# Attention with a batch's rounds of sums in one place, three exponentials a group, three score buffers in a fixed turn

## The chip, the cores and the metric

The kernel runs on one core of a Trainium2 chip. The metric is the device time of one execution in microseconds (us), lower is better. In the text PE or TensorE is the matrix engine, ACT or ScalarE does the exponentials, DVE or VectorE and POOL or GpSimd do element-wise work, and SP's queue issues most transfers.

## The reference

Attention for 8 batches of 12 heads, 448 positions, head size 64, with scores capped by a tanh; then a mixture of eight experts, each of which takes 448 of the 3584 tokens by a greedy assignment of the gate's logits.

```
scores = (q @ k.T) / 8
scores = cap * tanh(scores / cap)          # cap is 30
attn   = exp(scores - max);  attn /= sum(attn)
out    = attn @ v                          # per head; x = out as (3584, 768)
logits = x @ w_gate                        # 8 experts, at most 448 tokens each, in order of logit
y      = relu(x[mask] @ w1[e]) @ w2[e]     # per expert
```

## The kernel before, in words

All of it is one program whose order on every engine is written by hand: each engine carries out its instructions in the order in which the Python code emits them. Attention comes first (about the first 305 us), then the routing and the experts. The change touches attention only.

Attention goes through 24 **groups** g of four heads, three to a batch: b is the batch of the group and m (0, 1, 2) its place in it. One pass of the loop over g is a **step**. The 448 keys are cut into seven **blocks** r of 64. A step issues:

- `qk(g,r)`, in the order strings `Qr`: eight score matmuls (line 148) into a buffer `psS` of two PSUM banks, and a tanh on ACT (line 159) from there to a tile `e`. There are two such buffers. The exponential (line 164) works in place on `e`, one for the blocks (0,1), one for (2,3), one for (4,5) and one for block 6 (`GRP`); it is put behind the next block's tanh.
- `avq(g-1,r)`, `Ar`: eight matmuls (line 196) that multiply the weights of the group before by v and add up in `psA`, of which there is one. `av_out` (line 210) copies it to `xT` on DVE, and the next group's A0 waits for that copy.
- `esum`: DVE adds the `e` tiles of a group to `es` (line 170): `e1` at the end of the group's own step, `e2` and `r6` a step later. What is left are two halves; they are added by `r0` on DVE for the last group of a batch, and for the other two by `halves` on POOL (line 357), ahead of which a one-element copy `pin` (line 356) reads the newest `es`, so that it waits for DVE's sum.
- `rounds`: matmuls of `xT` with the gate's columns and of `es` with ones (line 219), 32 columns of the array each. They give the logits of batch b-1 and its sums. There are three rounds a batch: `R0` in step m=0, `R1` in step m=1, `R2` in step m=2 (for batch 0, four in the same three places).
- after the last round `logit_in` and `sums` (lines 254 to 264), a step later `ltr` (four transpositions on PE, line 290), `logit` (lines 301 to 309) on DVE and `heads` (line 326) on POOL.
- for the batch two back, `turn` (a DVE transposition, line 271) and `scale` (POOL, line 278), whose result goes to HBM.
- `tr`: two DVE transpositions that make the next group's `tk` and `tq` (line 133), without which its Q0 can't start.

`ORDER`, `EARLY`, `BEFORE` and `FINAL` (lines 348 to 351) say in which order blocks, rounds and the last batch's extra work (`T0`, `T4`, `W`, `L`) come. The small accumulators (`misc` and `side` of the rounds, the transposed logits) have two PSUM banks of their own, `psM`.

Of the kernel before, what the change touches and what calls it, by code (L numbers as in the profile page):

```python
# [8 lines left out]
PSUM=bass.MemoryType.PSUM  # L9
# [7 lines left out]
EB=3  # L17
def attention(nc, tc, c1, xp, pM, ep, nl, pT, q, k, v, cap, w_gate, xs, L1, ident, on_logits, on_turn, NDEF, setup, mark):

# [4 lines left out]
    N=B*NQ  # L24
# [23 lines left out]
    with ExitStack() as ctx:  # L48
# [4 lines left out]
        c2=ctx.enter_context(tc.tile_pool(name="c2",bufs=1))  # L53
        pS=ctx.enter_context(tc.tile_pool(name="pS",bufs=2,space=PSUM))

# [30 lines left out]
        nc.scalar.activation(tb,ident[:,0:1],AF.Tanh)  # L86
        ips=pM.tile([128,512],F32,name="psM")
        def idle(n):
# [41 lines left out]
        def tr(g,part,lo=0,hi=HG):  # L130
            if g>=N: return
            if lo==0: tks[g,part]=tp.tile([128,HG,S],F32,name="t"+"kq"[part])
            nc.vector.transpose(tks[g,part].rearrange("p m s -> p (m s)")[:,lo*S:hi*S],nats[g,part][:,lo*NB:hi*NB,:].rearrange("p k d -> p (k d)"))
        GRP=((0,1),(2,3),(4,5),(6,)); LOC={r:(gi,n) for gi,rs in enumerate(GRP) for n,r in enumerate(rs)}
        def ev(g,r):
# [4 lines left out]
        def qk(g,r):  # L140
            gi,n=LOC[r]
            if n==0: eh[g,gi]=ep.tile([128,len(GRP[gi]),2,S],F32,name=f"e{gi}")
            ps=pS.tile([128,2,512],F32,name="psS")
            if g:
                for o in range(2):
                    for h in range(2):
                        hp=slice(h*64,h*64+64)
                        nc.tensor.matmul(ps[o*64:o*64+64,h,:S],tks[g,0][hp,o,r*64:r*64+64],tks[g,1][hp,o,:],start=True,stop=True)  # L148
            elif r<6:
                o,u=divmod(r,3)  # L150
                for h in range(2):
                    hp=slice(h*64,h*64+64)
                    for c in range(2): nc.tensor.matmul(ps[c*64:c*64+64,h,:S],tks[g,0][hp,o,u*128+c*64:u*128+c*64+64],tks[g,1][hp,o,:],start=True,stop=True)
            else:
                for o in range(2):
                    for h in range(2):
                        hp=slice(h*64,h*64+64); w=64*(1-o)
                        nc.tensor.matmul(ps[w:w+64,h,:S],tks[g,0][hp,o,384:448],tks[g,1][hp,o,:],start=True,stop=True)
            nc.scalar.activation(ev(g,r),ps[:,:,:S],AF.Tanh,scale=sr[0])  # L159
            e=eh[g,gi]  # L160
            while wait: wait.pop(0)()
            if g==N-1 and gi>=2: e=ev(g,r)
            elif n<len(GRP[gi])-1: return
            act=lambda: nc.scalar.activation(e,e,AF.Exp,scale=sr[1],bias=bias)  # L164
            if g==N-1 and gi>=2: act()
            else: wait.append(act)
        def esum(g,what):
            if not 0<=g<N: return
            if what=='e1': es_t[g]=es.tile([128,2,2,S],F32,name="es",bufs=4)
            t=es_t[g]; add=lambda o,a,b: nc.vector.tensor_tensor(o,a,b,op=ALU.add)  # L170
            if g==0 and what in ('e1','e2'):
                o=int(what[1])-1
                add(t[:,o],ex(g,o,0),ex(g,o,1)); add(t[:,o],t[:,o],ex(g,o,2))
            elif g==0:
# [4 lines left out]
            elif what=='e1': add(t,eh[g,0],eh[g,1])
            elif what=='e2': add(t,t,eh[g,2])  # L180
            else:
                r=int(what[1])
                add(t[:,0],t[:,0],ev(g,r) if r else t[:,1])
        avp={}; pair=[None]
# [26 lines left out]
        def rnd(b,*ns,of=None):  # L211
            of=of or (ROUNDS if b else FIRST)
            for n in ns:
                for q,t,a,c,k in of[n]:
                    bank=(misc,side)[k]
                    if b not in bank: bank[b]=pM.tile([128,512],F32,name="psM")
                    rhs=xT[b][:,c,:] if t is gw else es_t[b*NQ+c[0]][:,c[1],c[2],:]
# [4 lines left out]
        def turn_v(lo,hi):  # L222
            if not lo:
# [3 lines left out]
                for o in range(2): nc.gpsimd.memset(vt['g'][o*64:o*64+64,:,:,16+o:17+o],1.0)  # L227
            ps=pM.tile([128,512],F32,name="psM")
            for r in range(lo,hi): nc.tensor.transpose(ps[:,(r-lo)*128:(r-lo+1)*128],nats[N-1,2][:,r].rearrange("p h d -> p (h d)"),ident)
            nc.vector.tensor_copy(vt['t'][:,lo*128:hi*128],ps[:,:(hi-lo)*128])  # L230
        def gate_v():
            ps=pM.tile([128,512],F32,name="psM")
            for r in range(7):
# [7 lines left out]
        def logit_v(b,of,t,under):  # L241
            lg=xp.tile([128,S],F32,name="lgt",bufs=1)
            nc.scalar.activation(lg,of[:,:S],AF.Copy)
            under()
            ps=pM.tile([128,512],F32,name="psM")
            for j in range(NJ): nc.tensor.matmul(ps[:CP,j*36:j*36+36],lg[:,j*CP:(j+1)*CP],fold,start=True,stop=True)
# [7 lines left out]
        def logit_in(b,p0=0):  # L254
            lgs[b]=xp.tile([128,S],F32,name="lg",bufs=1)
            nc.vector.tensor_copy(lgs[b][p0:],misc.pop(b)[p0:,:S])
            if b in side:
                nc.vector.tensor_tensor(lgs[b][64:],lgs[b][64:],side.pop(b)[:64,:S],op=ALU.add)
# [26 lines left out]
        def ltr(b,what=0,pool=None):  # L285
            p0=64 if what==2 else 0; W=128-p0
            lg=lgs.pop(b)
            ps=pM.tile([128,512],F32,name="psM") if pool is None else pool
            for j in range(NJ):
# [57 lines left out]
        part=None  # L347
        ORDER=["Q2 A0 Q3 Q4 A1 A2 A3 Q5 Q6 A4 A5 A6","Q2 R1 A1 Q3 Q4 A2 A3 Q5 Q6 A4 A5 A6","Q2 A1 A2 Q3 Q4 R2 A3 Q5 Q6 A4 A5 A6"]
        EARLY=["Q2 Q3 Q4 I2 Q5 I4 Q6 I16","Q2 A1 A2 Q3 Q4 Q5 A3 A4 Q6 A5 A6"]
        BEFORE="Q2 A1 Q3 R1 Q4 T0 A2 Q5 A3 A4 Q6 T4 A5 A6"  # L350
        FINAL="Q2 A1 R2 Q3 Q4 A2 L A3 Q5 A4 W Q6 A5 A6"
        HELD=lambda g: g==N-2 or 0<=g<N and 0<g//NQ<B-1 and g%NQ<2
        pin=c1.tile([1,1],F32,name="pin")
        def halves(g,last):
            if not HELD(g): return
            if last is not None: nc.gpsimd.tensor_copy(pin,es_t[last][0:1,0,0,0:1])
            nc.gpsimd.tensor_tensor(es_t[g][:,0],es_t[g][:,0],es_t[g][:,1],op=ALU.add)
        RNO=({"R0":(0,1),"R1":(2,),"R2":(3,)},{"R0":(0,),"R1":(1,),"R2":(2,)})
        def rounds(bb,m,n):
            rnd(bb,*RNO[bb>0][n])  # L360
            if m==2:
                logit_in(bb)
                if bb<B-NDEF: sums(bb)
        for g in range(N):
# [6 lines left out]
            last=g==N-1  # L371
            order=g>=G2; first=bb==0; old=bb-1 if m==0 and 0<=bb-1<B-NDEF else None
            qk(g,0)
            if old is not None: ltr(old)
            if m==0 and bb>=0: rounds(bb,m,"R0")
            qk(g,1)
            av_out(g-2)
            if g and (m or g<G2): avq(g-1,0)
            stored()
            if m: halves(g-4+m,g-1)  # L380
            if old is not None: logit(old); heads(old)
            if m==0 and bb>1: on_turn(bb-2)
            turn(b-2,m); scale(b-2,m)
            two=(0,1) if m==1 else (1,0)
            tr(g+1,two[0] if order else 0)
            if order: tr(g+1,two[1])
            if m==1 and bb>0: on_logits(bb-1)
            for w in ('e2','r') if g==1 else ('e2','r6'): esum(g-1,w)
            if g>1 and not HELD(g-1): esum(g-1,'r0')
            if last: halves(N-2,None)  # L390
            if not order: tr(g+1,1)
            for t in (EARLY[g] if g<2 else FINAL if last else BEFORE if g==N-2 else ORDER[m]).split():
                if t[0]=='R': bb>=0 and rounds(bb,m,t)
                elif t=='L': logit(bb); on_logits(bb)
                elif t[0]=='I': idle(int(t[1:]))
                elif t=='T0': turn_v(0,4)
                elif t=='T4': turn_v(4,7)
                elif t=='W': gate_v()
                else: (qk if t[0]=='Q' else lambda g,r: avq(g-1,r))(g,int(t[1]))
            if not last: esum(g,'e1')  # L400
        av_out(N-2)
        stored()
        g=N-1; b=B-1
        LAST=[RA,RB]
        two=pS.tile([128,2,512],F32,name="psS")
        part_v(two[:,0],0,1)
# [21 lines left out]
class Routing:  # L428
# [198 lines left out]
    def search(s,wp,turned=()):  # L627
# [473 lines left out]
def full(nc,tc,q,k,v,cap,wg,w1,w2,out):  # L1101
    with ExitStack() as ctx:
# [63 lines left out]
```

## Time and profile before

| what | value |
|---|---|
| three runs | 858.77, 858.78, 859.48 us; median 858.78 |
| the profiled execution | 858.0 us, its span from the first to the last instruction 856.2 |
| busy share of the span | PE 98%, DVE 68%, ACT 67%, POOL 54% |
| attention | about 0 to 305 us |

The shares are means over attention and experts. In attention ACT, DVE and PE are all near full. The profiled execution's own time (858.0) is 0.78 below the median of the runs. TensorE's granted clock is full in all of it.

### The profile page before, as it was taken

Reading aid. Unit: us, or ns where it says so; the run is one execution under the profiler, and the core shown is the slowest. Engines: PE = TensorE matmul, PEld = TensorE weight load, DVE = VectorE, ACT = ScalarE, POOL = GpSimd, SP = SyncE. Lnnn points to the kernel's source line nnn. Section 1 sums busy time; section 2 is a strip of 40 time slices with the busy share of each in tenths; the row PEclk is TensorE's granted clock in tenths of the full one; section 3 lists DMA queues with packets and bytes.
Section 4 is the critical chain, followed back from the end, with each engine's and each line's share of the span. In section 5 each row is a group of like instructions: output and inputs, shape, how many; then the busy total and the mean of one; then the engine's idle time right before and its main releaser. Section 6 shows DMA issues by size and latency. Waiting matters only on the chain.

```text
span 856.2 us, 17676 instructions
## 1 busy us (share of the span) xinstructions
PE 840.2 (98%) x6109; PEld 614.5 (72%) x6109; DVE 580.4 (68%) x1907; ACT 572.4 (67%) x832; POOL 462.5 (54%) x637
## 2 busy tenths in 40 slices
PE   8999999999999998999999999999999999999997
PEld 5333333333333357889889989989899899999997
DVE  3878899999989778667777777777757780230110
ACT  6999999999999753562764755737727725525521
POOL 8203336346333235573673864856856856837931
PEclk9999999999999999999999999999999999999999
DMA  8999999888995107716706917927928828838601
GB/s 126 137 142 148 157 158 156 159 160 158 154 152 125 23 2 226 229 36 189 222 16 193 311 42 209 317 58 207 308 56 211 288 65 232 257 118 234 202 10 56
DMA packets 364249, 133.70 MB, mean 156 GB/s; under 512 B 290592, under 2 KB 357472, under 8 KB 364160
## 3 DMA queue, kind: packets, MB, share of 16 engines
q1 hardware_dynamic: 354656, 102.27, 55.5%
q0 software_dynamic: 4656, 22.02, 7.5%
q10 hardware_dynamic: 4848, 8.29, 2.9%
q8 instruction: 48, 0.79, 0.4%
q14 instruction: 41, 0.34, 0.1%
HBM read 94.40 MB, written 30.08 MB: 145 GB/s over the span
## 4 chain that ended last, share of the span: by engine, by line
PE 76%; issue 7%; DVE 5%; SPq 5%; DMA 4%; POOL 2%; ACT 1%; POOLq 0%; ACTq 0%; DVEq 0%
PE psH L1002 25%; PE psH L1033 20%; PE psA L196 13%; PE psS L148 12%; SPq L83 3%; PE psM L219 2%; DVE es L170 2%; DMA xg<-xs,idx 1%; DVE cmpD L605 1%; POOL w2l L884 1%; DMA k<-in_k_dram 1%; DMA w1r<-in_moe_w_dram 1%; PE psX L826 1%; PE psM L290 1%; SPq L867 1%
## 5 line engine op out<-in xcount | busy, mean ns | idle before, releaser
L1033 PE MATMUL psH<-w2h,hh 128*128 128x384 f32 x896 | 235.3, 340 | 0.0
L1033 PE MATMUL psH<-w2l,hh 128*128 128x384 f32 x512 | 166.5, 340 | 0.5 <-POOL gap L882 0.5
L1033 PEld LDWEIGHTS psH<-w2h,hh 128*128 128x128 f32 x896 | 161.8, 188 | 0.3
L164 ACT ACTIVATE e<-e,bias 128x1792 f32<-128x1792 f32 (+1 forms) x97 | 158.5, 1636 | 0.1
L159 ACT ACTIVATE e<-psS 128x896 f32<-128x896 f32 x168 | 150.5, 956 | 11.1 <-PE psS L148 7.1
L1002 PE MATMUL psH<-xgh,w1h 128*128 128x448 f32 x384 | 143.2, 373 | 0.3 <-ACT xgh L962 0.3
L1002 PE MATMUL psH<-xgh,w1l 128*128 128x448 f32 x384 | 141.5, 369 | 0.0
L148 PE MATMUL psS<-tq,tk 64*64 64x448 f32 x1288 | 139.3, 538 | 1.1 <-ACT e L159 1.1
L884 POOL TENSOR_TENSOR w2l<-w2r,w2h 128x768 fp32r<-128x768 f32 x64 | 118.1, 1846 | 37.5 <-ACT w2h L880 30.5
L1002 PE MATMUL psH<-xgl,w1h 128*128 128x448 f32 x384 | 136.8, 369 | 0.0
L196 PE MATMUL psA<-e,nv 64*64 64x448 f32 x1232 | 131.9, 539 | 1.0 <-DVE xT L210 1.0
L884 POOL TENSOR_TENSOR w1l<-w1r,w1h 128x768 fp32r<-128x768 f32 x62 | 114.2, 1843 | 19.7 <-ACT w1h L880 15.3
L148 PEld LDWEIGHTS psS<-tq,tk 64*64 64x64 f32 x1288 | 47.5, 132 | 75.4 <-issue 47.0
L196 PEld LDWEIGHTS psA<-e,nv 64*64 64x64 f32 x1232 | 44.8, 133 | 73.8 <-issue 64.3
L1033 PEld LDWEIGHTS psH<-w2l,hh 128*128 128x128 f32 x512 | 95.6, 188 | 1.5 <-POOL gap L882 1.4
L1008 ACT ACTIVATE hh<-psH 128x448 fp32r<-128x448 f32 x64 | 34.8, 544 | 86.4 <-PE psH L1002 80.1
L1010 DVE SCALAR_TENSOR_TENSOR hh<-psH,hh 128x64 fp32r<-128x64 f32 (+1 forms) x128 | 44.0, 386 | 67.8 <-ACT hh L1008 66.7
L1039 ACT ACTIVATE on<-psH 128x384 f32<-128x384 f32 x48 | 23.4, 487 | 88.5 <-PE psH L1033 82.5
L170 DVE TENSOR_TENSOR es<-es,e 128x896 f32<-128x896 f32 (+2 forms) x48 | 77.7, 1619 | 2.5
L909 POOL DMA_INDIRECT xg<-xs,idx x32 | 34.3, 1073 | 81.2 <-DVE zz L774 64.8
L1002 PEld LDWEIGHTS psH<-xgh,w1h 128*128 128x128 f32 x384 | 72.5, 189 | 5.8 <-ACT xgh L962 0.5
L1002 PEld LDWEIGHTS psH<-xgh,w1l 128*128 128x128 f32 x384 | 72.3, 188 | 5.3
(390 smaller groups left out, 1339.1 us busy)
## 6 DMA issues: line engine op xcount, KB each, us to landing
w1r<-in_moe_w_dram SPq DMA_DIRECT2D x128, 192.0 KB, 4.7
w2r<-in_moe_w_dram SPq DMA_DIRECT2D x64, 384.0 KB, 6.5
k<-in_k_dram SPq DMA_DIRECT2D x92, 112.0 KB, 3.8
q<-in_q_dram SPq DMA_DIRECT2D x92, 112.0 KB, 4.0
nv<-in_v_dram SPq DMA_DIRECT2D x88, 112.0 KB, 3.3
xs<-xw SPq DMA_DIRECT2D x72, 112.0 KB, 2.6
xz<-pl ACTq DMA_DIRECT2D x18, 384.0 KB, 3.3
xs<-xn SPq DMA_DIRECT2D x1, 1344.0 KB, 6.5
```

The lines of the kernel that those rows point to most:

```text
L83: (nc.scalar if first and a else nc.sync).dma_start(z[w:w+32,lo*NB:hi*NB,:],src[b,h0+2*t+lo:h0+2*t+hi,:,a*32:a*32+32].rearrange("h (k s) d ...
L148: nc.tensor.matmul(ps[o*64:o*64+64,h,:S],tks[g,0][hp,o,r*64:r*64+64],tks[g,1][hp,o,:],start=True,stop=True)
L159: nc.scalar.activation(ev(g,r),ps[:,:,:S],AF.Tanh,scale=sr[0])
L164: act=lambda: nc.scalar.activation(e,e,AF.Exp,scale=sr[1],bias=bias)
L170: t=es_t[g]; add=lambda o,a,b: nc.vector.tensor_tensor(o,a,b,op=ALU.add)
L196: nc.tensor.matmul(avp[g,o][h*64:h*64+64,:S],z[hp,r,h,:],ev(g,r)[hp,h,:],start=r==0,stop=r==6)
L884: (eng or nc.gpsimd).tensor_tensor(view(l),r,view(h).bitcast(F32),op=ALU.subtract)
L909: g=nc.gpsimd.indirect_dma_start(out=row(j,n),out_offset=None,in_=xs,in_offset=bass.IndirectOffsetOnAxis(ap=res[p][0][:n,j:j+1],axis=0))
L1002: nc.tensor.matmul(ps[:,:C],a[:,c,:],b[:,c,:],start=(m==0),stop=(m==DC*3-1)); m+=1
L1008: nc.scalar.activation(h[:,:C],ps[:,:C],AF.Relu)
L1010: nc.vector.scalar_tensor_tensor(h[:,d:d+b-a],ps[:,a:b],0.0,h[:,a:b].bitcast(F32),op0=ALU.max,op1=ALU.subtract)
L1033: nc.tensor.matmul(ps[:,:HD],h[:,f,a:a+128],spl[p,2,hf,f//2][w][:,f%2,:],start=(m==0),stop=(m==nm-1))
```

## The change

Three PSUM buffers of two banks each (`ps1`, `ps2` and `psM`) are handed out in a fixed turn by `two_banks` to blocks Q, to the rounds and to the transposed logits alike; `misc` and `side` of a batch share one. The idle matmuls of the start write to `psA`. Exponentials are made for the blocks (0,1,2), (3,4) and (5,6). The sums of a group, now called P, S, C and r, are all made a step later. The halves are added on POOL for all three groups of batches 1 to 6, at the beginning of the step, without `pin`. All rounds of a batch stand in step m=1, and A5 and A6 of that step go to the beginning of the next. `ltr` (`T`) stays in step m=0. The order of everything else is in the strings as well.

```diff
-        pS=ctx.enter_context(tc.tile_pool(name="pS",bufs=2,space=PSUM))
+        pS=ctx.enter_context(tc.tile_pool(name="pS",bufs=1,space=PSUM))
+        def two_banks():
+            two_banks.n+=1
+            k=two_banks.n%3
+            return pS.tile([128,2,512],F32,name=f"ps{k}") if k else pM.tile([128,2,512],F32,name="psM")
+        two_banks.n=0
+        ring.append(lambda: two_banks()[:,0])
...
-        GRP=((0,1),(2,3),(4,5),(6,)); LOC={r:(gi,n) for gi,rs in enumerate(GRP) for n,r in enumerate(rs)}
+        GRP=((0,1,2),(3,4),(5,6)); LOC={r:(gi,n) for gi,rs in enumerate(GRP) for n,r in enumerate(rs)}
...
-            ps=pS.tile([128,2,512],F32,name="psS")
+            ps=two_banks()
...
-            if g==N-1 and gi>=2: e=ev(g,r)
+            if g==N-1 and gi==2: e=ev(g,r)
             elif n<len(GRP[gi])-1: return
             act=lambda: nc.scalar.activation(e,e,AF.Exp,scale=sr[1],bias=bias)
-            if g==N-1 and gi>=2: act()
+            if g==N-1 and gi: act()
             else: wait.append(act)
         def esum(g,what):
...
+            if what=='P':
+                if g: add(t,eh[g,0][:,0:2],eh[g,1])
+                else:
+                    for o in range(2): add(t[:,o],ev(g,3*o),ev(g,3*o+1))
+            elif what=='C': add(t[:,0],t[:,0],ev(g,2))
+            elif what=='r': add(t[:,0],t[:,0],t[:,1])
+            elif g: add(t,t,eh[g,2])
+            else:
+                add(t[:,1],t[:,1],ev(g,5))
                 e=ev(g,6)
                 for o in range(2):
                     w=slice(64*(1-o),128-64*o)
                     add(t[w,o],t[w,o],e[w])
...
-                    if b not in bank: bank[b]=pM.tile([128,512],F32,name="psM")
+                    if b not in misc:
+                        two=two_banks()
+                        for o,z in enumerate((misc,side)): z[b]=two[:,o]
...
-            ps=pM.tile([128,512],F32,name="psM") if pool is None else pool
+            ps=two_banks()[:,0] if pool is None else pool
...
-        ORDER=["Q2 A0 Q3 Q4 A1 A2 A3 Q5 Q6 A4 A5 A6","Q2 R1 A1 Q3 Q4 A2 A3 Q5 Q6 A4 A5 A6","Q2 A1 A2 Q3 Q4 R2 A3 Q5 Q6 A4 A5 A6"]
-        EARLY=["Q2 Q3 Q4 I2 Q5 I4 Q6 I16","Q2 A1 A2 Q3 Q4 Q5 A3 A4 Q6 A5 A6"]
-        BEFORE="Q2 A1 Q3 R1 Q4 T0 A2 Q5 A3 A4 Q6 T4 A5 A6"
-        FINAL="Q2 A1 R2 Q3 Q4 A2 L A3 Q5 A4 W Q6 A5 A6"
-        HELD=lambda g: g==N-2 or 0<=g<N and 0<g//NQ<B-1 and g%NQ<2
-        pin=c1.tile([1,1],F32,name="pin")
-        def halves(g,last):
+        ORDER=["Q0 h c T v l y k P S C r t x e A0 Q1 Q2 Q3 A1 A2 A3 Q4 Q5 A4 A5 A6 Q6",
+               "Q0 h c t P k o x S C r v Q1 A0 A1 Q2 Q3 A2 A3 Q4 Q5 R0 R1 R2 i A4 Q6",
+               "Q0 A5- A6- h c t x k v P C S r Q1 Q2 Q3 A0 A1 Q4 A2 Q5 A3 A4 A5 A6 Q6"]
+        EARLY=["Q0 Q1 k v Q2 Q3 Q4 I2 Q5 I4 Q6 I16","Q0 Q1 A0 k P C S v Q2 A1 A2 Q3 Q4 Q5 Q6 A3 A4 A5 A6","Q0 c Q1 A0 k v P C S r Q2 A1 A2 Q3 Q4 A3 Q5 Q6 A4 A5 A6"]
+        FINAL="Q0 A5- A6- h c t x P C S H Q1 Q2 A0 Q3 A1 Q4 A2 Q5 V Q6 A3 A4 L A5 W A6"
+        HELD=lambda g: g==N-2 or 0<=g<N and 0<g//NQ<B-1
+        def halves(g):
             if not HELD(g): return
-            if last is not None: nc.gpsimd.tensor_copy(pin,es_t[last][0:1,0,0,0:1])
             nc.gpsimd.tensor_tensor(es_t[g][:,0],es_t[g][:,0],es_t[g][:,1],op=ALU.add)
...
             stored()
+            for t in (EARLY[g] if g<G2 else FINAL if last else ORDER[m]).split():
+                if t[0]=='Q': qk(g,int(t[1]))
+                elif t[0]=='A': avq(g-1-(t[-1]=='-'),int(t[1]))
+                elif t[0]=='R': bb>=0 and rnd(bb,*RNO[bb>0][t])
+                elif t[0]=='I': idle(int(t[1:]))
+                elif t=='c': av_out(g-2)
+                elif t=='h': halves(g-2)
+                elif t=='H': halves(g-1)
+                elif t=='T': old is not None and ltr(old)
+                elif t=='l':
+                    if old is not None: logit(old)
+                elif t=='e':
+                    if old is not None: heads(old)
+                elif t=='y':
+                    if bb>1: on_turn(bb-2)
+                elif t=='t': turn(b-2,m)
+                elif t=='x': scale(b-2,m)
+                elif t in 'kv': tr(g+1,two[t=='v'])
+                elif t in 'PCS': esum(g-1,t)
+                elif t=='r': not HELD(g-1) and esum(g-1,t)
+                elif t=='o': bb>0 and on_logits(bb-1)
+                elif t=='i':
+                    if bb>=0:
+                        logit_in(bb)
+                        if bb<B-NDEF: sums(bb)
                 elif t=='L': logit(bb); on_logits(bb)
+                elif t=='V': turn_v(0,7)
                 elif t=='W': gate_v()
```

## Rows read from the trace of the kernel before

**Rows 1.** Busy time by engine in one batch's stretch, with clock and DMA

```profile
core 0: us, PE busy (x) PEld busy (x) DVE busy (x) ACT busy (x) POOL busy (x), PEclk, DMA share, GB/s
...
151.83:187.13 35.30, 35.30 (x368) 13.33 (x365) 32.65 (x32) 34.88 (x34) 13.89 (x15) 1.00 0.89 156
```

**Rows 2.** Chain of waits: start, duration, what; R0 of two batches

```profile
151.01 0.89 PE psM L219 x8
...
186.31 0.89 PE psM L219 x8
```

**Rows 3.** Timeline of PE in a batch: start, duration, engine, line, instruction, count

```profile
144.05 0.57 PE L219 MATMUL psM<-es,ones 128*32 128x448 f32 x2
...
144.94 0.98 PE L196 MATMUL psA<-e,nv 64*64 64x448 f32 x8
145.74 1.68 PE L148 MATMUL psS<-tq,tk 64*64 64x448 f32 x16
147.25 2.44 PE L196 MATMUL psA<-e,nv 64*64 64x448 f32 x24
149.50 0.93 PE L148 MATMUL psS<-tq,tk 64*64 64x448 f32 x8
150.36 0.65 PE L290 MATMUL psM<-ident,lg 128*112 128x128 f32 x4
150.94 0.57 PE L219 MATMUL psM<-xT,gw 128*32 128x448 f32 x2
```

**Rows 4.** Timeline of PE after the last step, two rounds-shaped blocks in a row

```profile
297.69 0.94 PE L240 MATMUL psS<-e,q 128*32 128x448 f32 x8
298.44 0.55 PE L219 MATMUL psM<-xT,gw 128*32 128x448 f32 x2
```

**Rows 5.** Timeline of ACT in a batch

```profile
135.63 1.80 ACT L159 ACTIVATE e<-psS 128x896 f32<-128x896 f32 x2
137.23 1.88 ACT L164 ACTIVATE e<-e,bias 128x1792 f32<-128x1792 f32 x1
...
139.74 1.11 ACT L164 ACTIVATE e<-e,bias 128x896 f32<-128x896 f32 x1
140.67 1.79 ACT L159 ACTIVATE e<-psS 128x896 f32<-128x896 f32 x2
```

**Rows 6.** Timeline of DVE in a batch

```profile
150.18 1.08 DVE L210 COPY xT<-psA 128x896 f32<-128x896 f32 x1
...
152.10 1.10 DVE L271 STREAM_TRANSPOSE x<-xT 128x896 f32<-128x896 f32 x1
...
155.11 3.71 DVE L170 TENSOR_TENSOR es<-es,e 128x1792 f32<-128x1792 f32 x2
...
177.49 3.18 DVE L170 TENSOR_TENSOR es<-es,e 128x1792 f32<-128x1792 f32 x2
```

**Rows 7.** Timeline of POOL in the same batch

```profile
152.33 1.39 POOL L326 TENSOR_TENSOR lt<-lt 112x192 f32<-112x192 f32 x3 [1.09 <-DVE lt L309]
...
154.01 1.74 POOL L278 TENSOR_TENSOR xw<-x,R 128x896 f32<-128x896 f32 x1
...
162.09 2.09 POOL L357 TENSOR_TENSOR es<-es 128x896 f32<-128x896 f32 x1
```

**Rows 8.** Timeline of DVE in the second step

```profile
23.34 1.11 DVE L133 STREAM_TRANSPOSE tk<-k 128x896 f32<-128x896 f32 x1 [2.67 <-PE psS L148]
...
28.71 1.10 DVE L133 STREAM_TRANSPOSE tq<-q 128x896 f32<-128x896 f32 x1
```

**Rows 9.** Timeline of PE: Q0 of group 2, Q0 of the last group, its L

```profile
31.51 1.68 PE L148 MATMUL psS<-tq,tk 64*64 64x448 f32 x16
...
281.02 1.68 PE L148 MATMUL psS<-tq,tk 64*64 64x448 f32 x16
...
289.84 0.62 PE L290 MATMUL psM<-ident,lg 128*112 128x128 f32 x4 [0.93 <-DVE lg L258]
...
296.16 0.96 PE L240 MATMUL psS<-e,q 128*32 128x448 f32 x8
```

**Rows 10.** Timeline of DVE in the last step

```profile
290.50 0.36 DVE L301 RECIPROCAL rin<-psM 112x32 f32<-112x32 f32 x1 [0.80 <-PE psM L290]
...
295.17 0.39 DVE L235 COPY q<-psM 128x224 f32<-128x224 f32 x1
```

More of the change, by code (lines that the diff above doesn't have):

```diff
@@ L17, with attention @@
 EB=3
-def attention(nc, tc, c1, xp, pM, ep, nl, pT, q, k, v, cap, w_gate, xs, L1, ident, on_logits, on_turn, NDEF, setup, mark):
+def attention(nc, tc, c1, xp, pM, ep, nl, pT, q, k, v, cap, w_gate, xs, L1, ident, on_logits, on_turn, NDEF, setup, mark, ring):
     B,H,S,D=q.shape
@@ L86, in attention @@
         nc.scalar.activation(tb,ident[:,0:1],AF.Tanh)
-        ips=pM.tile([128,512],F32,name="psM")
+        ips=pT.tile([128,2,512],F32,name="psA",bufs=1)[:,0]
         def idle(n):
@@ L168, in esum @@
             if not 0<=g<N: return
[L169 to L174, printed above, removed]
+            if what=='P': es_t[g]=es.tile([128,2,2,S],F32,name="es",bufs=4)
+            t=es_t[g]; add=lambda o,x,y: nc.vector.tensor_tensor(o,x,y,op=ALU.add)
+            if what=='P':
[7 more added lines that the diff above has]
+                add(t[:,1],t[:,1],ev(g,5))
                 e=ev(g,6)
@@ L178, in esum @@
                     add(t[w,o],t[w,o],e[w])
[L179 to L183, printed above, removed]
         avp={}; pair=[None]
@@ L227, in turn_v @@
                 for o in range(2): nc.gpsimd.memset(vt['g'][o*64:o*64+64,:,:,16+o:17+o],1.0)
-            ps=pM.tile([128,512],F32,name="psM")
+            ps=two_banks().rearrange("p o s -> p (o s)")
             for r in range(lo,hi): nc.tensor.transpose(ps[:,(r-lo)*128:(r-lo+1)*128],nats[N-1,2][:,r].rearrange("p h d -> p (h d)"),ident)
@@ L231, in gate_v @@
         def gate_v():
-            ps=pM.tile([128,512],F32,name="psM")
+            ps=two_banks()[:,0]
             for r in range(7):
@@ L244, in logit_v @@
             under()
-            ps=pM.tile([128,512],F32,name="psM")
+            ps=two_banks()[:,0]
             for j in range(NJ): nc.tensor.matmul(ps[:CP,j*36:j*36+36],lg[:,j*CP:(j+1)*CP],fold,start=True,stop=True)
@@ L256, in logit_in @@
             nc.vector.tensor_copy(lgs[b][p0:],misc.pop(b)[p0:,:S])
-            if b in side:
+            if b<B-1:
                 nc.vector.tensor_tensor(lgs[b][64:],lgs[b][64:],side.pop(b)[:64,:S],op=ALU.add)
@@ L347, in attention @@
         part=None
-        ORDER=["Q2 A0 Q3 Q4 A1 A2 A3 Q5 Q6 A4 A5 A6","Q2 R1 A1 Q3 Q4 A2 A3 Q5 Q6 A4 A5 A6","Q2 A1 A2 Q3 Q4 R2 A3 Q5 Q6 A4 A5 A6"]
-        EARLY=["Q2 Q3 Q4 I2 Q5 I4 Q6 I16","Q2 A1 A2 Q3 Q4 Q5 A3 A4 Q6 A5 A6"]
-        BEFORE="Q2 A1 Q3 R1 Q4 T0 A2 Q5 A3 A4 Q6 T4 A5 A6"
-        FINAL="Q2 A1 R2 Q3 Q4 A2 L A3 Q5 A4 W Q6 A5 A6"
-        HELD=lambda g: g==N-2 or 0<=g<N and 0<g//NQ<B-1 and g%NQ<2
-        pin=c1.tile([1,1],F32,name="pin")
-        def halves(g,last):
+        ORDER=["Q0 h c T v l y k P S C r t x e A0 Q1 Q2 Q3 A1 A2 A3 Q4 Q5 A4 A5 A6 Q6",
[5 more added lines that the diff above has]
+        def halves(g):
             if not HELD(g): return
-            if last is not None: nc.gpsimd.tensor_copy(pin,es_t[last][0:1,0,0,0:1])
             nc.gpsimd.tensor_tensor(es_t[g][:,0],es_t[g][:,0],es_t[g][:,1],op=ALU.add)
         RNO=({"R0":(0,1),"R1":(2,),"R2":(3,)},{"R0":(0,),"R1":(1,),"R2":(2,)})
[L359 to L363, printed above, removed]
         for g in range(N):
@@ L371, in attention @@
             last=g==N-1
[L372 to L378, printed above, removed]
-            stored()
[L380 to L393, printed above, removed]
+            old=bb-1 if m==0 and 0<=bb-1<B-NDEF else None
@@ new lines, in attention @@
+            two=(0,1) if m==1 or g<G2 else (1,0)
+            stored()
+            for t in (EARLY[g] if g<G2 else FINAL if last else ORDER[m]).split():
[23 more added lines that the diff above has]
+                        if bb<B-NDEF: sums(bb)
@@ L394, in attention @@
                 elif t=='L': logit(bb); on_logits(bb)
-                elif t[0]=='I': idle(int(t[1:]))
-                elif t=='T0': turn_v(0,4)
-                elif t=='T4': turn_v(4,7)
+                elif t=='V': turn_v(0,7)
                 elif t=='W': gate_v()
-                else: (qk if t[0]=='Q' else lambda g,r: avq(g-1,r))(g,int(t[1]))
-            if not last: esum(g,'e1')
         av_out(N-2)
@@ L404, in attention @@
         LAST=[RA,RB]
-        two=pS.tile([128,2,512],F32,name="psS")
+        two=two_banks()
         part_v(two[:,0],0,1)
@@ L638, in search @@
             late=[lambda: s.propose_b(s.NC-4,s.NC,PB(nc)),lambda: None,lambda: s.key(s.NC-4,s.NC)]
-            post=lambda: s.flips(s.pm.tile([128,512],F32,name="psM"))
+            post=lambda: s.flips(s.pm.tile([128,2,512],F32,name="psM")[:,0])
         else: late,post=s.turns()
@@ L1112, in full @@
         xp=xctx.enter_context(tc.tile_pool(name="xp",bufs=2,side="right"))
-        pM=xctx.enter_context(tc.tile_pool(name="pM",bufs=2,space=PSUM,side="right"))
-        r.psum=lambda: pM.tile([128,512],F32,name="psM")
+        pM=xctx.enter_context(tc.tile_pool(name="pM",bufs=1,space=PSUM,side="right"))
+        ring=[]
+        r.psum=lambda: ring[0]()
         turned=set()
@@ L1127, in full @@
         pT=late.enter_context(tc.tile_pool(name="pT",bufs=1,space=PSUM,side="right"))
-        deferred,tail=attention(nc,tc,cp,xp,pM,ep,nl,pT,q,k,v,cap,wg,xs,L1,ident,on_logits,on_turn,NDEF,(r.indices,r.setup),r.mark)
+        deferred,tail=attention(nc,tc,cp,xp,pM,ep,nl,pT,q,k,v,cap,wg,xs,L1,ident,on_logits,on_turn,NDEF,(r.indices,r.setup),r.mark,ring)
         wp=ctx.enter_context(tc.tile_pool(name="wp",bufs=2))
```

## The prediction

> **What bounds the kernel now.** I read the page first for the shares, then the sums by stretch, because the shares mix attention with the experts. In one full batch of attention, 35.30 us long, PE is busy all the time, ACT for 34.88, DVE for 32.65, POOL for 13.89 [rows 1]. Three engines are within three microseconds of each other, so the order on each counts. Which of them bounds is seen in the timeline of PE: each block of eight matmuls begins 0.75 us after the one before it (145.74 to 149.50 is five blocks of 0.752), with no wait between [rows 3]. The batch adds up from PE's rows alone. 42 blocks of 0.752 are 31.58; three rounds of 0.89 (144.05 to 144.94) are 2.67; the block ahead of a round takes 0.86 in place of 0.75, the one behind it 0.80, so each change to the rounds' shape and back costs another 0.16, three times, 0.48; the transposed logits take 0.58 (150.36 to 150.94) [rows 3]. The sum is 35.31. The same round comes again after 35.30 in the chain of waits [rows 2]. So PE sets the pace in the batches, without loss, and what saves PE time there shows in full as long as nobody else becomes late.
>
> **The rounds in one place.** Inside the rounds' shape a block costs 0.75: of two in a row the second begins 0.75 after the first (297.69 to 298.44) [rows 4]. Three rounds in a row are then 0.75 + 0.75 + 0.89, with one change of 0.16: 2.55. The transposed logits, until now next to R0, stand alone and need a change of their own: 0.58 + 0.16 = 0.74. A batch becomes 31.58 + 2.55 + 0.74 = 34.87 on PE, 0.44 less than 35.31. There are six such batches (1 to 6 being summed, steps 6 to 23), 2.6 us. Batch 0 has four rounds in three places; together they save two changes of shape, some 0.5.
>
> **Three exponentials a group.** An exponential over two blocks takes 137.23 to 139.74 less one tanh, 2.51 - 0.80 = 1.71; one over a single block 0.93; a tanh is half of 1.60 [rows 5]. Two single ones would be 1.86, so an instruction saved is about 0.17 us: one over three blocks is 1.71 + 0.93 - 0.17 = 2.47. ACT's work in a batch falls by 3 x 0.17 = 0.5 to about 34.2, still under PE's 34.87. On the batches' path I cost it at nothing. PE's 34.87 covers it; if that were gone it would be worth 0.5 a batch, and it only keeps ACT from becoming the bound at once.
>
> **Three buffers.** A block's buffer comes back after the tanh of the third block before it, no longer the second. I followed the turn through a batch with these durations. ACT's tanh begins about 1.0 after its block; the tightest buffers of the batch are those that a round or the transposed logits hold: the block three places behind `T` needs DVE's `logit` (wanted at 3.8 us of the step, done at about 2.6), that behind the rounds needs `logit_in`. No wait as long as DVE is in time. So value nothing, from 0 to the next part's price.
>
> **DVE and POOL: who is late next.** DVE loses one half-sum a batch (1.0 us) to POOL: 31.6 of work for 34.87. Against this stands a lock between the two. Two sums of DVE take 3.18 when POOL is quiet and 3.71 when POOL's `scale` runs into them [rows 6]: that `scale` ran from 154.01 to 155.75 [rows 7], and the sum begun at 155.11 was longer by 0.53, as if it had begun when `scale` ended. A transposition beside `heads` (152.10, 1.10) keeps its length [rows 6]. The Trainium skill, "SBUF — State Buffer", section "Who interferes with whom", says the same as a rule: a DVE instruction with two SBUF inputs and a GpSimd instruction that reads SBUF can't run together, the one that issued first blocks the other. By that rule every half-sum that meets P, C or S costs its whole remaining length, as the row has it.
>
> Before, `pin` let `halves` start only when DVE's sum was through. Now `pin` is gone and a third half-sum a batch (2.09 [rows 7]) comes to POOL. Work a batch through from the rows, with times from Q0 of step m=0, unhindered starts of the steps at 0, 11.27, 22.85 and 34.87. In step m=0, DVE does c (1.0), v, l (0.92: c and l are 150.18 to 152.10), k, P, S, C, t, transpositions at 1.0 (152.10 to 155.11 is three) [rows 6]. It ends near 9.8. POOL's `scale` waits for t: 9.8 to 11.5; `heads` follows, 1.68 (152.33 to 154.01) [rows 7], to 13.2; the half-sum is queued behind it on POOL. DVE in step m=1: c at 10.8 (when A6 is done), t, then P at 12.9 once a piece of `heads` is through; the half-sum gets its turn behind P, 15.1 to 17.1; S wants 15.9 and starts at 17.1, until 19.05; `scale` then holds up C until 20.7; v ends at 22.7. Q0 of the next step needs v's result at 22.85. So the 3 us of locks use up the whole slack. In step m=2 `scale` delays P by 0.9, S ends 0.6 after the step, c of the next step is late, and A0 waits 0.2.
>
> Going on like this, batch by batch: the batches in which the routing's logits are prepared in step m=1 (`o`, 1.6 us more on DVE, groups 9 to 11 and 15 to 17) lose 1.15 and 0.15, the three others before the last 0, 0.2 and 0.2: 1.7 together. In the last batch r is still done on DVE in step m=1, v comes 0.95 late. I take 2.65 for all of them. The ends are 0 (in every batch the pieces fit) and 6.7 (each of five loses the 1.15 of the worst, and the last 0.95).
>
> **The start.** In steps 0 to 3 ACT and DVE set the pace. Step 1 now makes six sums of one block between k and v, before it was four: from 23.34 to 28.71 are a transposition and four sums, 1.08 a sum [rows 8]. v starts at about 30.9 and Q0 of group 2 at 32.1, where it was at 31.51 [rows 9]. From there PE, with three buffers, has no wait until step 3, and Q0 of group 3 comes out at 42.6, as before. Then A0 waits twice for the copy to `xT`, some 0.7 each, where before it was one such wait. With batch 0's saving of 0.5 the start comes out at 0.15 late; bounds -0.7 and +0.9.
>
> **The last step.** Before, it took from 281.02 to 296.16, 15.14, R2 of 1.05 among it [rows 9]. Now it has two more A blocks and seven transpositions of v in one place, no round. `L` needs the buffer of Q5, whose tanh comes behind an exponential over three blocks (2.47) and one over two (1.71): L at 12.2. From L to the end of DVE's copy for `W` it was 289.84 to 295.56 [rows 9, 10], 5.7, so the first product of the tail begins at 18.0 behind Q0, though PE has been done at 15.2. Before, the two came out within 0.6 of each other.
>
> **The sum.** With PE unhindered, Q0 of the step of group 5 comes at 66.96 (67.26 before), eighteen steps of the batches are 6 x 34.87 = 209.2, Q0 of the last step is at 276.2 (before: 281.02, with 1.4 of v's transpositions in it), the tail begins at 294.2 in place of 296.16: -2.0. The locks give back 2.65. In all +0.65 on the profiled execution's 858.0; all that follows, routing and experts, hangs on the end of attention and is shifted alike. That execution lies 0.78 below the median of the runs (858.78), so the same shift on the median gives 859.4.
>
> **The rivals.**
> - *The locks take back what the rounds give* (the forecast): 859.4. For it: the 3.71 against 3.18 [rows 6], and the slack of step m=1, 0.1 us. Against: my turns of DVE and POOL are exact to some 0.2 us only. Its own range is 857.2 to 861.2.
> - *The locks fall into slack*: v and c are always in time. Then -2.0 holds, 856.8; with the better end of the start 855.9. It decides at step m=1: v done before Q0 of the step behind it. For it: DVE has 31.6 of work for 34.87, and POOL's work of step m=0 might start earlier than I have it.
> - *DVE becomes the bound*: each batch loses v's 0.95 and c's 0.2, as the worst one does above. 6.7 - 2.0 = +4.7, 863.5. It decides when locks exceed 3.3 us a batch (34.87 - 31.6); I count 3 to 4. Before, no batch lost time to DVE [rows 1].
>
> **How the numbers follow.** A measurement of this kernel can tell about 0.2%, 1.7 us, from no change. The forecast has 0.41, the locks in slack 0.33, DVE as the bound 0.26. The likeliest case gives 859.4. The range runs from the second case with a good start (855.8) to just under the third (863.2). Faster by over 0.2%, below 857.1: the second case and little of the first, less its upper edge, 0.33. Within: most of the first, 0.40. Slower, above 860.5: the third and the edge of the first, 0.27.
>
> **What would show it.** In the profile after: R0 to R0 34.9 us apart if PE is unhindered, 35.3 or more if not; rounds 0.75 apart; ACT's three-block exponential 2.4 to 2.5. In PE's waits, if I am right: blocks of step m=2 waiting for `tk`/`tq` of DVE line 133, and A0 waiting for `xT`; DVE's sums of two blocks longer than 2.1, beside `halves` and `scale` on POOL. A gap of some 2.5 us on PE ahead of the tail, ended by DVE's copy for `W`. It would be wrong if POOL's half-sums ran in c and t, or if ACT, with 0.7 us of slack a batch, had to wait for more than that and PE then for its tanh.

## The result, and the profile after

The changed kernel takes 865.1 us (six runs, 864.29 to 866.19), the one before 858.77 (858.25 to 861.16). The ratio is 1.0071, interval 1.0056 to 1.0085: slower by some 6 us. The forecast was 859.4 in 855.8 to 863.2. It lies 1.9 outside that, on the side of the third rival (863.5). The profiled execution of after takes 864.93 with a span of 863.2, 6.9 more than before's.

Where the time went is read by putting the starts of the same TensorE block side by side. Each number is a start in PE's timeline, in us; the two columns at the right are runs told of below.

| Block | before | after | no half-sums | fastest run |
|---|---|---|---|---|
| Q0, group 6 | 78.83 | 79.48 | 78.79 | 79.50 |
| Q0, group 9 | 114.13 | 114.37 | 113.65 | 114.36 |
| Q0, group 12 | 149.50 | 150.06 | 148.51 | 149.43 |
| Q0, group 15 | 184.80 | 185.92 | 183.38 | 185.04 |
| Q0, group 18 | 220.10 | 221.56 | 218.24 | 219.91 |
| Q0, group 21 | 255.80 | 257.57 | 253.16 | 255.35 |
| Q0, group 23 | 281.02 | 282.55 | 275.99 | 278.19 |
| tail (`part_v`) | 296.16 | 300.78 | 294.18 | 294.01 |
| first expert product | 347.57 | 353.78 | 346.70 | 344.65 |
| last expert product | 851.38 | 858.28 | 850.73 | 848.96 |

The batches of after last 34.89, 35.69, 35.86, 35.64 and 36.01. Only the first is close to the 34.87 of the forecast. PE's timeline of after, where before had no wait [rows 3]; the bracket is the idle time ahead and what ended it:

```profile
169.16 0.57 PE L227 MATMUL ps<-xT,gw 128*32 128x448 f32 x2
...
169.94 0.55 PE L227 MATMUL ps<-xT,gw 128*32 128x448 f32 x2
...
170.70 0.55 PE L227 MATMUL ps<-xT,gw 128*32 128x448 f32 x2
...
171.55 0.98 PE L202 MATMUL psA<-e,nv 64*64 64x448 f32 x8
172.36 0.93 PE L154 MATMUL psM<-tq,tk 64*64 64x448 f32 x8
173.88 0.98 PE L154 MATMUL ps<-tq,tk 64*64 64x448 f32 x8 [0.59 <-DVE tq L139]
...
282.55 0.98 PE L154 MATMUL ps<-tq,tk 64*64 64x448 f32 x8 [1.74 <-DVE tq L139]
...
300.78 1.23 PE L248 MATMUL psM<-e,q 128*32 128x448 f32 x8 [2.44 <-DVE q L243]
...
303.21 1.73 PE L248 MATMUL psM<-e,q 128*32 128x448 f32 x8
```

The rounds stand in a row, 0.78, 0.76 and 0.85 apart. Q0 of step m=2 (173.88) waits for VectorE's v, so does Q0 of the last step, and the tail waits for the copy for `W`, where before began at 296.16 without a wait [rows 9]. Why v is late stands in the timelines of DVE and of POOL in the same stretch of after (at 165.99 two sums in one row, the first of 5.59):

```profile
163.06 1.98 DVE L176 TENSOR_TENSOR es<-e,e 128x1792 f32<-128x1792 f32 x1
164.97 1.10 DVE L139 STREAM_TRANSPOSE tk<-k 128x896 f32<-128x896 f32 x1
165.99 6.71 DVE L176 TENSOR_TENSOR es<-es,e 128x1792 f32<-128x1792 f32 x2
172.62 1.10 DVE L139 STREAM_TRANSPOSE tq<-q 128x896 f32<-128x896 f32 x1
```

```profile
165.92 2.10 POOL L364 TENSOR_TENSOR es<-es 128x896 f32<-128x896 f32 x1
167.96 1.74 POOL L286 TENSOR_TENSOR xw<-x,R 128x896 f32<-128x896 f32 x1
```

S and C took 3.18 before when POOL was quiet [rows 6]; here 6.71. The half-sum began 0.07 ahead of S, `scale` followed it without a break, and S ended 1.9 behind both, about as long as it takes alone. S met this pair four times, in groups 7, 13, 19 and 22, and took 4.80, 5.59, 5.11 and 5.58 us. At group 7 it cost nothing: v was done at 102.18 and Q0 started at 102.33. In the two batches with the routing's proposal (step m=1, groups 10 and 16) the half-sum met the proposal's first comparison instead (112x64, 1.85 us), and S took 2.02. The Trainium skill, "SBUF — State Buffer", section "Who interferes with whom", says that the second to issue blocks fully until the first is done. For S and the half-sum the trace agrees; but `scale` began 1.97 after S and was through before it, so the wait can be for two instructions.

Busy time by engine, first a batch of after beside [rows 1], then the stretch behind the tail's wait:

```profile
core 0: us, PE busy (x) PEld busy (x) DVE busy (x) ACT busy (x) POOL busy (x), PEclk, DMA share, GB/s
150.06:185.92 35.86, 35.16 (x368) 14.63 (x364) 35.01 (x30) 34.65 (x30) 15.50 (x14) 1.00 0.99 166
...
302.00:304.00 2.00, 2.00 (x15) 0.57 (x9) 0.00 (x0) 0.00 (x0) 0.00 (x0) 0.50 0.00 0
```

DVE went from 32.65 to 35.01 of a batch: it is now the fullest engine but PE. An instruction counts as busy here while it stands and waits for the other engine, as S does for 3.6 us of them. And behind the tail's wait the granted clock was 0.50, the lower level (1.2 GHz), for some 3 us: the blocks at 301.72 and 303.21 took 1.49 in place of 0.75.

ScalarE's three-block exponential, where before had two instructions [rows 5], takes 2.42 from start to start:

```profile
156.01 2.56 ACT L170 ACTIVATE e<-e,bias 128x2688 f32<-128x2688 f32 x1
158.43 0.94 ACT L165 ACTIVATE e<-ps 128x896 f32<-128x896 f32 x1
```

### The profile page after: what moved, and what is told of

The parts are those of the page before. It is cut to its first block, busy times and chain, and to the rows that moved or that the text cites. A ratio compares the mean times of both kernels' runs of the same rounds, so it can differ in the third digit from the quotient of the medians.

```text
span 863.2 us, 17618 instructions
## 1 busy us (share of the span) xinstructions
PE 839.4 (97%) x6109; PEld 625.6 (72%) x6109; DVE 591.3 (68%) x1900; ACT 568.8 (66%) x808; POOL 471.4 (55%) x631
## 4 chain that ended last, share of the span: by engine, by line
PE 56%; DVE 15%; issue 9%; SPq 8%; DMA 7%; POOL 3%; ACT 2%; POOLq 0%; DVEq 0%
PE psH L1006 23%; PE psH L1037 20%; DVE es L176 5%; PE psA L202 5%; SPq L89 5%; DMA q<-in_q_dram 3%; PE ps L154 3%; DMA xs<-xw 2%; DVE tq L139 1%; PE psX L830 1%; SPq L290 1%; PE psM L154 1%; DVE cmpD L609 1%; DVE tk L139 1%; DVE x L279 1%
## 5 line engine op out<-in xcount | busy, mean ns | idle before, releaser
L170 ACT ACTIVATE e<-e,bias 128x1792 f32<-128x1792 f32 (+2 forms) x73 | 148.9, 2039 | 0.1
L888 POOL TENSOR_TENSOR w2l<-w2r,w2h 128x768 fp32r<-128x768 f32 x64 | 118.1, 1846 | 37.7 <-ACT w2h L884 27.0
L165 ACT ACTIVATE e<-ps 128x896 f32<-128x896 f32 x112 | 101.0, 933 | 12.1 <-PE ps L159 5.1
L154 PE MATMUL ps<-tq,tk 64*64 64x448 f32 x856 | 96.7, 537 | 2.9 <-DVE tq L139 2.7
L202 PEld LDWEIGHTS psA<-e,nv 64*64 64x64 f32 x1232 | 49.2, 133 | 67.6 <-issue 62.3
L176 DVE TENSOR_TENSOR es<-es,e 128x896 f32<-128x896 f32 (+2 forms) x48 | 87.1, 1817 | 2.4
L1006 PEld LDWEIGHTS psH<-xgl,w1h 128*128 128x128 f32 x384 | 72.3, 189 | 5.3
```

Of the source, the lines that this page charges most:

```text
L176: t=es_t[g]; add=lambda o,x,y: nc.vector.tensor_tensor(o,x,y,op=ALU.add)
L202: nc.tensor.matmul(avp[g,o][h*64:h*64+64,:S],z[hp,r,h,:],ev(g,r)[hp,h,:],start=r==0,stop=r==6)
L888: (eng or nc.gpsimd).tensor_tensor(view(l),r,view(h).bitcast(F32),op=ALU.subtract)
L1006: nc.tensor.matmul(ps[:,:C],a[:,c,:],b[:,c,:],start=(m==0),stop=(m==DC*3-1)); m+=1
```

## The experiments

**GpSimd's half-sums left out of the changed kernel.**

```
 def halves(g):
-    if not HELD(g): return
+    return
```

> The changed kernel without GpSimd's half-sums: the two halves of a group's sums are not added together, so the sums that the rounds use are incomplete; all else is as in the changed kernel. Theory L (GpSimd's half-sums and scale keep VectorE's two-input sums waiting, so v comes late for Q0 and c late for A0): S beside POOL falls from 5.59 us to under 4, the batches from 35.6-36.0 to 34.9-35.1, Q0 of the last step comes some 4 to 5 us earlier, 865.1 becomes about 859.5. Rival B (the fixed turn of three score buffers makes TensorE wait) and rival W (VectorE simply has too much of its own work): batches and time unchanged, 865.

859.13 us, ratio to before 1.0007 (0.9997 to 1.0016). The batches are 34.86, 34.86, 34.87, 34.86 and 34.92, and the tail begins at 294.18: the forecast's batch of 34.87 and its unhindered tail at 294.2. DVE's busy time in a batch falls to 32.23:

```profile
148.51:183.38 34.87, 34.87 (x369) 13.76 (x364) 32.23 (x30) 34.38 (x30) 9.62 (x11) 1.00 1.03 161
```

The longest S and C of DVE's timeline beside POOL are now this pair, 1.3 over its quiet length:

```profile
164.24 4.52 DVE L176 TENSOR_TENSOR es<-es,e 128x1792 f32<-128x1792 f32 x2
```

Buffers (B) and VectorE's own work (W) are as in the changed kernel, so theory L stands. Subtracting the columns of the table gives its price: the two differ by 0.69 at group 6 (and by as much at group 5, ahead of the first half-sum) and by 6.60 at the tail, so 5.9 us. The medians differ by 6.0.

**The same work in another order**, VectorE's transpositions and copies beside GpSimd's instructions:

```
-ORDER=["Q0 h c T v l y k P S C r t x e A0 ...", "Q0 h c t P k o x S C r v Q1 ...",
+ORDER=["Q0 h c T t x l v y e k P S C r A0 ...", "Q0 h c t x k v o P S C r Q1 ...",
```

> The changed kernel with the same operations in another order in the first two steps of a batch: VectorE's transpositions and copies (l, v, k, t, x) stand first, so that they run beside GpSimd's scale, heads and half-sum, and the sums P, S, C come when GpSimd is through. Theory L (it is the meeting of VectorE's sums with GpSimd's instructions that costs): S falls to some 2 to 3 us, batches 34.9 to 35.1, about 859.5 to 860.5. Rivals B (buffers) and W (amount of work on VectorE): 865, batches 35.6 to 36.0.

861.08 us, 1.0028 (1.0017 to 1.0039): 4 of the 5.9 come back, with no work removed; theory L had expected 0.6 to 1.6 more to come back. Three batches take 34.86 to 35.12; two still lose over 1 (35.99 and 36.28). They are those that follow a batch with the routing's proposal, whose delay DVE carries on until A0 waits for `xT`:

```profile
152.71 0.98 PE L202 MATMUL psA<-e,nv 64*64 64x448 f32 x8 [1.05 <-DVE xT L216]
```

**The half-sums on VectorE instead.**

```
-HELD=lambda g: g==N-2 or 0<=g<N and 0<g//NQ<B-1
+HELD=lambda g: g==N-2
```

> The changed kernel with the half-sums on VectorE (r behind S) in place of GpSimd, but for group N-2; the work of the computation is all there. VectorE was busy for 32.5 of 35 us without half-sums and 34.1 with those on GpSimd; three half-sums of 1.09 make 35.8 of 35. Theory L (a half-sum on GpSimd costs VectorE about 0.5 by the lock, its own work costs 1.09): VectorE becomes the bound, batches 35.8 to 36.5, 866 to 871. Rival (locks cost more than the work itself, so that VectorE is better off): batches 35.0 to 35.5, 860 to 863.

869.61 us, 1.0124 (1.0108 to 1.0141). VectorE is the bound: 35.75 busy of 36.45. Even with its lock, a half-sum is cheaper on GpSimd.

```profile
152.77:189.22 36.45, 35.17 (x369) 14.59 (x365) 35.75 (x33) 34.83 (x30) 9.25 (x11) 1.00 0.92 158
```

In this run the tail waits as in the changed kernel, for 2.44, yet the granted clock behind the wait stays at 1.00. So a wait of this length isn't always followed by the low clock. PE's timeline, then the stretch behind it:

```profile
305.17 0.96 PE L248 MATMUL psM<-e,q 128*32 128x448 f32 x8 [2.44 <-DVE q L243]
```

```profile
305.17:308.00 2.83, 2.83 (x32) 1.25 (x36) 0.85 (x1) 0.00 (x0) 0.00 (x0) 1.00 0.00 0
```

**The kernel before without `pin`.**

```
 def halves(g,last):
     if not HELD(g): return
-    if last is not None: nc.gpsimd.tensor_copy(pin,es_t[last][0:1,0,0,0:1])
```

> The kernel before without pin: GpSimd's half-sum may start as soon as its sums are done. Theory L (the meeting of half-sum and VectorE's sums costs): VectorE's sums get longer beside the half-sum, 0 to 3 us slower, by how much slack VectorE has there; rival (half-sums cost nothing, or it is the number of them): 858.6, unchanged.

868.16 us, 1.0105 (1.0089 to 1.0120). L expected the sign, but at most 3 of the 9.3. DVE's timeline, then POOL's, then PE's:

```profile
121.76 5.42 DVE L170 TENSOR_TENSOR es<-es,e 128x1792 f32<-128x1792 f32 x2
127.21 1.09 DVE L170 TENSOR_TENSOR es<-es 128x896 f32<-128x896 f32 x1
128.22 2.02 DVE L170 TENSOR_TENSOR es<-e,e 128x1792 f32<-128x1792 f32 x1
130.15 1.08 DVE L210 COPY xT<-psA 128x896 f32<-128x896 f32 x1
```

```profile
122.35 3.88 POOL L356 TENSOR_TENSOR es<-es 128x896 f32<-128x896 f32 x1
```

```profile
131.29 0.98 PE L196 MATMUL psA<-e,nv 64*64 64x448 f32 x8 [1.19 <-DVE xT L210]
```

The half-sum waits for one sum, then the next sum waits for it: 5.42 where the same pair took 3.71 [rows 6]. Of these 1.7 some 1.4 go on, through the copy to `xT`, to PE, and a batch becomes 36.72 (116.27 to 152.99). PE waits for this copy for 1.2 to 1.7 in every batch.

**Rounds in one place, in the kernel before.**

```
-ORDER=["Q2 A0 ...","Q2 R1 A1 Q3 Q4 A2 A3 Q5 Q6 ...","Q2 A1 A2 Q3 Q4 R2 A3 ..."]
+ORDER=["Q2 A0 ...","Q2 A1 Q3 Q4 A2 A3 Q5 R0 R1 R2 Q6 ...","Q2 A1 A2 Q3 Q4 A3 ..."]
```

(Its edit also takes R0 from its place in step m=0 and moves `T0` and `T4` to the last step.)

> The kernel before with one part of the change: batches 1 to 6 do their three rounds in one place of step m=1 (and v's transpositions move to the last step). Theory (a change of matmul shape costs TensorE 0.16 us, and the rounds alone bring what the prediction counted): 0.44 less a batch, batches 34.9, about 855.5 to 856. Rival (VectorE's logit_in and sums behind all rounds come late in a step that has no slack): part of it is eaten by waits, 857 to 859.

874.03 us, 1.0172 (1.0158 to 1.0186). The rounds take what was forecast (0.78, 0.75, 0.87), yet the batch is 37.7. DVE does `logit_in` and its sums at the end of step m=1, ahead of the group's next sum and the copy to `xT`, and A0 waits 1.2 for that copy in every batch. Further blocks begin 0.1 to 0.5 late. One in a batch waits 0.29 for ACT's tanh (160.90); what the others wait for is not settled.

**Three exponentials, in the kernel before.**

```
-GRP=((0,1),(2,3),(4,5),(6,))
+GRP=((0,1,2),(3,4),(5,6))
```

(The sums take their blocks from the new groups.)

> The kernel before with one other part alone: three exponentials a group, of 3, 2 and 2 blocks, two score buffers as before. Theory (ScalarE is not on the path): no change, 858.0 to 859.0. Rival (an exponential of 2.4 us holds up the tanh behind it, and two score buffers don't cover that): TensorE waits for ScalarE's tanh in every group, up to 0.5 us each, 860 to 870.

898.3 us, 1.046 (1.0446 to 1.0474), 28 above the rival's upper end. With two buffers PE stands still while an exponential holds up the next tanh, three times a batch, and twice more for the copy to `xT`. PE's timeline:

```profile
139.29 0.98 PE L148 MATMUL psS<-tq,tk 64*64 64x448 f32 x8 [0.51 <-ACT e L159]
144.83 0.98 PE L196 MATMUL psA<-e,nv 64*64 64x448 f32 x8 [0.80 <-DVE xT L210]
153.39 0.98 PE L148 MATMUL psS<-tq,tk 64*64 64x448 f32 x8 [1.26 <-ACT e L159]
```

A batch becomes 40.8 (88.66 to 129.45). The changed kernel has none of these waits for ACT in its batches. That its third buffer hides the longer exponential is read from this; no run adds that buffer alone.

**The last step: the copy for `W` ahead of the proposal.**

```
-elif t=='L': logit(bb); on_logits(bb)
+elif t=='L': logit(bb)
 ...
 av_out(N-2)
+on_logits(bb)
```

> The changed kernel with the proposal of the last batch's logits (on_logits) issued behind av_out(N-2) instead of within L, so that on VectorE the copy for W comes ahead of it. Theory (the wait ahead of the tail is VectorE's queue: the proposal stands ahead of the copy): the 2.44 us wait of part_v goes, and with it the low clock behind it, 1.7; the proposal comes later and may give back 0.7: about 861.5. Rival (the tail waits for the proposal's result anyway, in the routing behind it): the gap moves behind the tail, 864 to 865.5.

861.61 us, 1.0038 (1.0025 to 1.0051), as expected. The wait is gone and the clock stays at 1.00:

```profile
299.45 0.96 PE L248 MATMUL psM<-e,q 128*32 128x448 f32 x8
```

From Q0 of the last step to the first expert product it takes 66.9 in place of 71.2. Of these 4.3 some 1.2 are lost at the start: in this execution the granted clock was 0.50 from 33 to 36 us, behind a wait of 2.06 ahead of Q0 of group 2, and Q0 of group 3 came at 45.02 (42.73 in the changed kernel). The run with the half-sums on VectorE has the same there (0.50 from 34 to 37, Q0 at 45.01), while the fastest run waits 2.54 at that place and keeps the full clock; what decides it isn't known.

**Idle products inside that wait**, in the changed kernel and in the reordered one:

```
 two=two_banks()
+for _ in range(10): nc.tensor.matmul(two[:,1,:128],ident,ident,start=True,stop=True)
 part_v(two[:,0],0,1)
```

> The changed kernel with ten idle products of the identity issued on TensorE ahead of part_v, while it waits for VectorE's copy for W. Theory K (behind the 2.44 us wait the granted clock falls, 0.67 in 300 to 304 us, and the first blocks of the tail take up to 1.49 us in place of 0.75): the idle products sit inside the wait, the clock stays at 1.0, blocks stay at 0.75, tail 1.7 us shorter, 863.4. Rival (those blocks are slow because of their operands or of somebody else's use of memory): blocks stay at up to 1.49, 865.

865.04 us, 1.0072 (1.0059 to 1.0085): no gain. The mechanism is there. Clock of the same stretch:

```profile
302.00:304.00 2.00, 2.00 (x28) 0.91 (x24) 0.00 (x0) 0.00 (x0) 0.00 (x0) 1.00 0.00 0
```

The tail begins at 300.84, its blocks take 0.75, and the experts start at 351.58, 2.2 earlier than in the changed kernel. The lead holds past 700 us and is lost in the sixth and seventh of the eight experts to three waits of 0.6 (724, 783 and 787) that the changed kernel's trace does not have; the last product begins only 0.3 earlier. From the first expert product to the end it takes 511.2 here, and 508.6 to 509.4 in every other trace.

> The run with GpSimd beside the transpositions alone (861.1; its tail came 3.6 us later than in the run with the other last step, its experts 6.2 later) with ten idle products ahead of part_v. Theory K (of those 6.2, 2.6 are the granted clock that fell behind the wait): start of the tail unchanged, granted clock 1.0 behind it, experts 2 to 2.6 earlier, 858.5 to 859. Rival (as in the first run with idle products, the end of the program is set by something in the experts that doesn't move): experts earlier, time 861.

860.66 us, 1.0018 (1.0008 to 1.0029), against 861.08 (intervals overlap); the rival's 861 is nearer than theory K's 859. In the profiled execution the experts start 2.4 earlier and the lead is kept to the end, but that of the run it is set against was its slowest (863.17). What the low clock costs in the end stays open: some 2 us by the traces of this run and of the copy put first, nothing that can be told by the medians of the two with idle products.

**Towards a version that beats both.** First the reordered batches with another last step:

```
-FINAL="Q0 A5- A6- h c t x P C S H Q1 ... Q5 V Q6 A3 A4 L A5 W A6"
+FINAL="Q0 L A5- A6- h c P C S H Q1 ... Q5 V p t x Q6 A3 A4 A5 W A6"
```

> As the run with GpSimd beside the transpositions (861.1), with another order in the last step too: the logits of the last batch first, then the sums, the proposal behind v's transpositions, so that VectorE's copy for W is early. If the wait ahead of the tail (2.44) and the low clock behind it (about 2) hang on VectorE's queue in the last step, both go: 856.5 to 857.5. If the tail then waits for the proposal: 859 to 861.

857.21 us, 0.998 (0.9971 to 0.9989). The tail begins at 294.70. Then, on top of it, two edits, each in a run of its own:

```
-"Q0 h c t x k v o P S C r Q1 ... R2 i A4 Q6", "Q0 A5- A6- h c t x ..."
+"Q0 h c t x k v P S C r o Q1 ... R2 H i A4 Q6", "Q0 A5- A6- c t x ..."
```

> The fastest run so far (857.2) with the proposal of the logits (o) behind the sums in step m=1, and the half-sum of step m=0's group at the end of step m=1 in place of the start of m=2. Theory L (what is left of the batches' waits, 0.34 and 1.0 us, is a sum of the proposal, 1.65 beside scale, and P, 2.8 beside scale): those waits go, 1 to 1.5 less, about 856. Rival (in those batches VectorE simply has too much work): waits of the same size elsewhere, 857.2, or more where logit_in behind the proposal comes late.

855.82 us, 0.9967 (0.9957 to 0.9978), the fastest, though its interval just overlaps that of the run it builds on. The waits of 221 to 225 us went down to 0.1; that of A0 at 151 became 0.69 (0.34). Two things were moved at once, and which of them did it isn't told apart.

> The fastest run so far (857.2) with P ahead of the transpositions of k in steps 2 and 3, so that the sums are done while VectorE waits for the loads of k and q. If the waits of 1.0 at 45 us and 0.1 at 57 us are a copy to xT that is late behind the sums: both go, 1 less, about 856.2. If ScalarE sets the pace of those steps: 857.2.

(Its edit: `P` ahead of `k` in steps 2 and 3.) 857.34 us, 0.9984 (0.9976 to 0.9993). The wait at 45 us fell from 1.0 to 0.46, but the time did not move by an amount that can be told.

## Why the prediction was wrong

- **PE as the bound, and the rounds:** right. Without half-sums the batch is 34.87 and the tail begins at 294.18, against 34.87 and 294.2. That the tail agrees to 0.02 is chance: Q0 of group 5 came 0.2 earlier and the last step took 0.2 longer than forecast.
- **Exponentials:** 2.42, forecast 2.47. Their cover was misnamed: put alone into the kernel before, with its two buffers, they cost 39 us and not 0.5 a batch, as PE waits for a tanh behind them. So it isn't PE's 34.87 that covers them but, by these waits, the third buffer, and the **three buffers**, "value nothing", are what this part stands on. ACT's work was summed wrongly: 34.88 less 0.5 is 34.4, not 34.2. Without half-sums it measured 34.38, so the slack was 0.5 and not 0.7; it was enough.
- **The start:** Q0 of group 2 was forecast at 32.1 and came at 32.18; in the runs with the same first two steps it lies between 31.63 and 33.08, so a cost of 0.15 can't be told. The two waits for the copy to `xT`, forecast at 0.7 each, were 1.00 and 0.40.
- **DVE and POOL: the step that failed.** I counted 2.65; by the run without half-sums it is 5.9. From group 6 on the batches lost 0.03, 0.83, 0.99, 0.78 and 1.09, the last steps 2.2, where I had 0, 1.15, 0.2, 0.15, 0.2 and 0.95. The sum is off by 3.3. That the engines lock each other out, where it hurts (v, Q0 of step m=2) and its witnesses were as written; what failed is the order of the turns, and with it the size. I let the two engines take turns: S behind the half-sum, C behind `scale`, 2.8 in all, and v done at 22.7 of the batch, just in time. In the trace `scale` follows the half-sum and S waits for both (3.6 over its own length). In the batch shown v is done at 23.7. So two of the three batches without a proposal, which I had nearly free, lose as much as those with one, and the last steps lose twice what I had: 3.0 of the 3.3 stand there. The bound that I gave, 6.7, holds it. The third rival's condition (locks of over 3.3 a batch) was met by S and P alone, 3.6 and 0.7 in the batch shown, and its price was the nearer one.
- **The last step:** right to 0.2: the tail began 18.2 behind Q0 (forecast 18.0), PE waited 2.44 (2.5).
- **What I left out:** the clock behind that wait. From the tail to the first expert product it took 53.0 in place of 51.4; another 0.7 came in the experts, where the traces of other runs differ as much. Such a wait doesn't always bring the clock down: the run with the half-sums on VectorE had the same one at full clock.
- **The sum** for the profiled execution: -2.0 unhindered, 5.9 of locks, 0.7 at the start (against the run without half-sums, whose start was the earliest of all), 1.6 at the clock and 0.7 in the experts make 6.9, which is what it lost.

## What to carry to other kernels

Where VectorE and GpSimd both read memory, lay out which of VectorE's instructions stand beside each of GpSimd's, and put transpositions and copies there: that alone was worth 4 us here. When pricing such a meeting, count as the dear end that a sum waits for everything that GpSimd has queued, not for one instruction. And ask of each part of a change what hides it: rounds, exponentials and `pin` each cost 9 to 39 us when changed alone in the old kernel.

## What the runs showed that was not expected

GpSimd's instructions on 112x8 elements, which the proposal issues, took 1.97 us beside VectorE's sums and 0.20 without: a small instruction of GpSimd stands as long as the sum of 2.0 that it meets. POOL's timeline of the reordered run, then of the fastest:

```profile
133.66 1.97 POOL L560 TENSOR_SCALAR r_Bt<-r_b 112x8 f16<-112x8 int32 x1 [0.25 <-DVE r_c L555]
```

```profile
138.14 0.20 POOL L561 TENSOR_SCALAR r_Bt<-r_b 112x8 f16<-112x8 int32 x1 [4.67 <-DVE r_c L556]
```

Which engine gets in next is not always the same. GpSimd kept on in the four meetings above; in the reordered run, at 123.30, VectorE's sum got in between `scale` and a piece of `heads`, which then took 2.38.
